# Filler matmuls kept to the first microseconds, other places for two early loads, and value rows copied from on-chip tiles

## The chip, the cores and the metric

The kernel runs on one core of a Trainium2 chip. The metric is the device time of one execution in microseconds (us); three executions of the kernel before took 718.28, 718.65 and 720.03 us, so its median is 718.65 us. The core has a matrix engine (PE, whose weight loads are listed apart as PEld), a vector engine (DVE), a scalar engine (ACT), a general engine (POOL) and a queue engine (SP), which issues nearly all the transfers (DMAs) between memory and the chip here. Each engine takes its own instructions strictly in the order in which they were written; semaphores order the engines against each other.

## The reference

Local attention with a few global keys is followed by a gated two-layer network. Shapes: 4 batches, 8 heads, 768 positions, 64 elements in a head; 8 global keys and a window of 96; then 3072 tokens of 512 elements, with 2048 hidden elements.

```python
scores = scale * q @ k^T                       # per batch and head
keep   = (pos_k < n_global) | (0 <= pos_q - pos_k < n_local)
bias   = -slope[head] * (n_local if global and not local else |pos_q - pos_k|)
a      = softmax(where(keep, scores + bias, -1e9))
x      = (a @ v) as [3072, 512]
h      = x @ w_in                              # w_in, w_out are float64 in memory
out    = (h * sigmoid(h)) @ w_out
```

Only keys in the window and the first 8 count, so a block of 128 queries needs its own 128 keys, the 96 before them and the 8 global ones: 232 columns, or 128 for the first block of a batch.

## The kernel before

The work is cut into 24 blocks of 128 queries (6 a batch) and each block into 4 pairs of heads. Two blocks form a group of 256 tokens, which goes through the network in 16 steps of 128 hidden elements; so there are 12 groups. Keys and queries of a block are loaded as rows and turned on PE (L464, "tq"), and ACT copies the turned halves out of PSUM to KHw and QHw (L534, L536). POOL copies the key columns that two blocks share (L544, L546). For each pair of heads PE makes the scores (L557 in the first 6 blocks, L529 later), DVE adds the bias and takes the extreme (L567), ACT takes the exponential and its sum (L575), DVE makes the inverse and scales (L582 to L591), PE turns the result (L605), ACT copies it out (L619), and PE multiplies by the values (L633). ACT and DVE split the attention's output in a high and a low part (xh L651, xl L654).

The network's weights come as 64-bit floats. They are staged in 32 pieces (even numbers w_in, odd ones w_out, L380), and DVE makes 32-bit floats of each with three passes over bits (L384, L390, L396) and, after ACT's high part (L403), a low part (L407). The network is then three matmuls for every product, high by high, high by low and low by high (L769 for w_in, L794 for w_out), with ACT and DVE between them (L775, L779, L783, L787). The groups 0 and 1 go through the network while the weights are still being converted. Blocks 6 and later wait for the last piece of weights.

The order of all instructions on all engines is laid down before the program is built, by a list planner (class Plan). It keeps a clock of its own with costs given by hand, takes the ready operation of lowest rank on each engine, and checks room in the pools: 3 buffers of tag "qkn" (rows of keys and queries), 3 of "big" (staged weights, later outputs), 2 each of "vn" and "vp" (values). What it writes down is a fixed order. Where its PE has nothing ready before its time WEND and a PSUM bank is free, it writes a filler, a 128x256 bf16 matmul of zeros whose result nobody reads (L905). Up to its time COLD it counts every PE cost twice.

The values that a block needs from the block before it (96 rows) and of the global keys (8 rows) are in a tile of their own, vp, filled by two DMAs (L456, L459) from v in memory. The block's own values are in vn (L449).

Of the kernel before, what the change touches and what calls it, by code (L numbers as in the profile page):

```python
# [21 lines left out]
P = 128  # L22
NPREV = 96
NG = 8
WIN = NPREV + NG + P
C1 = NPREV + NG
# [1 line left out]
FAR = 1.0e9  # L28
PAR = dict(

    LAT=140, SD=125, DL=1900, D0=2700, DW=2900, DO=3400, MG=60, T2=45000, LAT2=230, MG2=400, F0=600, F1=1200, C1=900, C2=2300, COLD=5200, WEND=60000,

    CAP=dict(po=4, av=2, s=4, h=3, tp=2, tq=4), HU=13,

    C0=14, CR=1, LW=1, LB=5, QB=3.5, RI=0.1, RN=0, RP=0.2, RM=0, RV=1.2, RQ=0.1, RB=3, LK=-25, LAG=1,

    BP=(4, 3), NX=20, CF=2, AHEAD=5, SB=(4,), CN=4, I0=6, QS='ACT',
)


# [130 lines left out]
def attn_moe(ctx, tc, q, k, v, n_global, n_local, w_in, w_out, out):  # L171
    nc = tc.nc
# [4 lines left out]
    NJ = S // P  # L177
# [148 lines left out]
    op = plan.op  # L326
# [113 lines left out]
    blk = [dict() for _ in range(B * NJ)]  # L440
    xt = {}

    def load(i, nm, h0=0, h1=H):
        b, j = divmod(i, NJ)
        pool, tag = (sb2, "vn") if nm == "v" else (sb3, "qkn")
        if not h0:
            blk[i][nm] = pool.tile([P, H, D], F32, name=f"{nm}n", tag=tag)
        src = dict(k=k, q=q, v=v)[nm]
        nc.sync.dma_start(  # L449
            blk[i][nm][:, h0:h1], src[b, h0:h1, j * P:(j + 1) * P, :].rearrange("h p d -> p h d")  # L450
        )

    def load_prev(i):
        b, j = divmod(i, NJ)
        blk[i]["vp"] = x = sb2.tile([C1, H, D], F32, name="vp")
        nc.sync.dma_start(  # L456
            x[:NPREV], v[b, :, j * P - NPREV:j * P, :].rearrange("h p d -> p h d")
        )
        nc.sync.dma_start(x[NPREV:], v[b, :, :NG, :].rearrange("h p d -> p h d"))  # L459

    def turn(i, nm, tp, p0=0, p1=NHP):
        blk[i]["t", nm, p0] = ps = bank(tp, NHP, P)
# [199 lines left out]
    before = {}  # L662
    for i in range(B * NJ):
# [13 lines left out]
                        later.append(o)  # L677
                    ob[nm + "h", p0, p1] = op("ACT", 51 + 107 * n, rank, (lambda nm=nm, a=p0, b=p1: high(0, nm, a, b)), [o], [tp, hi])
        for nm in "kq" if i else "":
            xn, tp = Buf("qkn"), Buf("tq")  # L680
            hi, lo = kk[nm.upper() + "H"], kk[nm.upper() + "L"]
            o = op("DMA", 1456, rank - lr, (lambda i=i, nm=nm: load(i, nm)), (), [xn], PAR["DL"])
            if i == PAR["I0"]:
                before["lent"] = before["move"]
            o = op("PE", 440, rank, (lambda i=i, nm=nm, tp=tp: turn(i, nm, tp)), [o, before.get("lent")], [xn, tp, hi] if whole(i) else [xn, tp, hi, lo])
            if i >= PAR["I0"]:
                hs = [op("ACT", 500, rank, (lambda i=i, nm=nm, a=a: stack_high(i, nm, a, False)), [o], [tp, x])
                      for a, x in enumerate((hi, lo))]
                for a, x in enumerate((hi, lo)):
                    y = x if nm == "k" else kk["R"]  # L690
                    ob[nm, a] = op("DVE", 718, rank, (lambda i=i, nm=nm, a=a: stack_low(i, nm, a)),
                                   hs + ([o_wf] if nm == "q" else []), [tp, x, y])
                    if nm == "q":
                        ob[nm, a, 2] = op(
                            "ACT", 640, rank + PAR["RQ"], (lambda i=i, a=a: twin_low(i, a)), [ob[nm, a]], [y]
                        )
                        ob[nm, a, 1] = op(
                            PAR["QS"], dict(ACT=628, POOL=1930, DVE=335)[PAR["QS"]], rank + PAR["RQ"],
                            (lambda i=i, nm=nm, a=a: stack_high(i, nm, a, True)), [hs[a]], [x]
                        )  # L700
                continue
            ob[nm + "h"] = op("ACT", 583 if nm == "q" else 470, rank, (lambda i=i, nm=nm: high(i, nm)), [o], [tp, hi])
# [9 lines left out]
                    )  # L712
        o_v = [op("DMA", 1456, rank - lr + 1, (lambda i=i: load(i, "v")), (), [kk["vn"]], PAR["DL"])]
        if j:
            o_v.append(op("DMA", 1183, rank - lr + 1, (lambda i=i: load_prev(i)), (), [kk["vp"]], PAR["DL"]))
        pav = Buf("av")
        last, o_m, pts = None, [], []
        for hp in range(NHP):
# [362 lines left out]
```

## Time and profile before

| What | us |
|---|---|
| median of three executions | 718.65 |
| the profiled execution | 718.39 |
| its span, first to last instruction | 716.4 |
| PE busy | 708.4 |
| DVE busy | 475.8 |
| ACT busy | 419.2 |

Around the span lie 2.0 us of the profiled execution. The page's slices of a fortieth (17.9 us) show DVE at 6 tenths in the first, 9 in the next six and 7 to 8 in the three after; from the eleventh slice on it is at 5 to 7 tenths until the last fifth. PE has 9 tenths or more in all slices but the last. A matmul's end in the trace is modelled and consecutive matmuls overlap, and fillers count as busy, so PE's share is not a share of useful work. In a window row "PE 2.00 (x12)" is busy time in that stretch and the number of instructions; in the chain of waits a row is start, length and what held the chain then; in a timeline row the bracket is the engine's idle time before and what ended it.

### The profile page before, as it was taken

What the parts mean: (1) busy time and instruction counts of PE and PEld (TensorE: products, weight loads), DVE (VectorE), ACT (ScalarE), POOL (GpSimd) and SP (SyncE); (2) the same over time, 40 slices, a digit from 0 to 9 for tenths busy, and PEclk for the clock granted to TensorE, in tenths of its full rate; (3) what the DMA queues carried; (4) which work ended last, traced back from release to release, by engine and by line L of the source; (5) the groups of instructions that cost most, each with busy time, mean ns of one, the idle gap of its engine ahead of it and who ended that gap; (6) DMA issues with size and microseconds to landing.
All of it is one profiled execution on the core that took longest, in us unless ns stands there. A gap on an engine that the chain in (4) does not pass through costs nothing.

```text
span 716.4 us, 14026 instructions
## 1 busy us (share of the span) xinstructions
PE 708.4 (99%) x5165; PEld 632.7 (88%) x5165; DVE 475.8 (66%) x1489; ACT 419.2 (59%) x1092; POOL 25.2 (4%) x83
## 2 busy tenths in 40 slices
PE   9999999999999999999999999999999999999996
PEld 7778999889999999999999998999899999998985
DVE  6999999787666757666666666665675766543332
ACT  5977444596656647556566575665664756443221
POOL 2000000010000000000000000000000000000000
PEclk9999999999999999999999999999999999999999
DMA  8895546252413305124123142240431412000001
GB/s 160 225 278 151 173 131 193 70 149 59 116 45 101 87 30 145 46 71 128 48 76 104 43 115 73 73 115 16 118 85 32 130 31 57 30 1 1 30 1 34
DMA packets 117215, 63.95 MB, mean 89 GB/s; under 512 B 93460, under 2 KB 110100, under 8 KB 117140
## 3 DMA queue, kind: packets, MB, share of 16 engines
q1 hardware_dynamic: 116992, 62.86, 32.8%
q8 instruction: 42, 0.69, 0.4%
q14 instruction: 33, 0.27, 0.1%
q10 hardware_dynamic: 148, 0.13, 0.1%
HBM read 56.69 MB, written 6.29 MB: 88 GB/s over the span
## 4 chain that ended last, share of the span: by engine, by line
PE 95%; DVE 3%; ACT 1%; issue 0%; ACTq 0%
PE bank L769 38%; PE bank L794 38%; PE bank L633 5%; PE bank L605 5%; PE bank L529 4%; PE bank L464 3%; PE bank L905 1%; PE bank L557 1%; DVE pe L591 1%; DVE pe L567 1%; ACT pe L575 1%; DVE xl L654 0%; DVE rs L582 0%; DVE wf L390 0%; DVE wf L396 0%
## 5 line engine op out<-in xcount | busy, mean ns | idle before, releaser
L769 PE MATMUL bank<-xh,WIH 128*128 128x256 f32 x768 | 224.2, 292 | 0.0
L769 PE MATMUL bank<-xl,WIH 128*128 128x256 f32 x768 | 216.1, 281 | 0.0
L769 PE MATMUL bank<-xh,WIL 128*128 128x256 f32 x768 | 215.0, 280 | 0.0
L769 PEld LDWEIGHTS bank<-xh,WIH 128*128 128x128 f32 x768 | 144.6, 188 | 10.0 <-issue 3.1
L769 PEld LDWEIGHTS bank<-xl,WIH 128*128 128x128 f32 x768 | 144.7, 188 | 6.4
L769 PEld LDWEIGHTS bank<-xh,WIL 128*128 128x128 f32 x768 | 144.8, 189 | 0.0
L794 PE MATMUL bank<-WOH,gh 128*128 128x512 f32 x336 | 135.5, 403 | 0.0
L775 ACT ACTIVATE th<-bank 128x256 f32<-128x256 f32 x192 | 73.6, 383 | 104.8 <-PE bank L769 96.2
L794 PE MATMUL bank<-WOH,gl 128*128 128x512 f32 x336 | 132.4, 394 | 0.0
L794 PE MATMUL bank<-WOL,gh 128*128 128x512 f32 x336 | 132.1, 393 | 0.0
L783 ACT CAST gh<-th 128x256 fp32r<-128x256 f32 x192 | 77.3, 402 | 83.1 <-PE bank L794 63.9
L779 DVE SCALAR_TENSOR_TENSOR th<-th,bank 128x256 f32<-128x256 f32 x192 | 80.9, 421 | 57.6 <-ACT th L775 55.6
L787 DVE TENSOR_TENSOR gl<-th,gh 128x256 fp32r<-128x256 f32 x192 | 82.0, 427 | 51.9 <-ACT gh L783 48.0
L575 ACT ACTIVATE pe<-pe,NM 128x232 f32<-128x232 f32 (+1 forms) x192 | 90.6, 473 | 32.9 <-DVE NM L567 31.1
L567 DVE CUSTOM_DVE_ANT_0 pe<-bank,B 128x232 f32<-128x232 f32 (+1 forms) x192 | 68.6, 376 | 54.6 <-PE bank L529 52.4
L794 PEld LDWEIGHTS bank<-WOH,gl 128*128 128x128 f32 x336 | 63.1, 188 | 15.2
L794 PEld LDWEIGHTS bank<-WOH,gh 128*128 128x128 f32 x336 | 63.4, 189 | 7.2 <-issue 0.5
L794 PEld LDWEIGHTS bank<-WOL,gh 128*128 128x128 f32 x336 | 63.4, 189 | 6.8
L619 ACT COPY pt<-bank 128x512 f32<-128x512 f32 (+1 forms) x80 | 43.8, 549 | 29.5 <-PE bank L605 29.2
L591 DVE TENSOR_SCALAR pe<-pe,rs 128x232 f32<-128x232 f32 (+1 forms) x192 | 56.3, 330 | 1.6
L605 PE MATMUL bank<-ident,pe 128*128 128x128 f32 (+1 forms) x352 | 55.0, 275 | 0.0
L427 DVE TENSOR_REDUCE TOP<-c 128x1 f32<-128x512 int16 x64 | 42.8, 681 | 12.2 <-DMA c<-in_moe_w_in_dram 12.2
(126 smaller groups left out, 883.2 us busy)
## 6 DMA issues: line engine op xcount, KB each, us to landing
c<-in_moe_w_in_dram SPq DMA_DIRECT2D x16, 512.0 KB, 4.8
c<-in_moe_w_out_dram SPq DMA_DIRECT2D x16, 512.0 KB, 3.9
vn<-in_v_dram SPq DMA_DIRECT2D x24, 256.0 KB, 3.7
w<-in_moe_w_in_dram SPq DMA_DIRECT2D x12, 512.0 KB, 4.7
w<-in_moe_w_out_dram SPq DMA_DIRECT2D x12, 512.0 KB, 3.6
kn<-in_k_dram SPq DMA_DIRECT2D x23, 256.0 KB, 3.7
qn<-in_q_dram SPq DMA_DIRECT2D x23, 256.0 KB, 3.1
out_dram<-osb SPq DMA_DIRECT2D x23, 256.0 KB, 2.8
```

Of the source, the lines that this page charges most:

```text
L427: nc.vector.tensor_reduce(TOP[:, i, n:n + 1], top, AX.X, (ALU.min, ALU.max)[i], apply_absolute_value=True)
L567: nc.vector.tensor_tensor_reduce(t["p", hp][:, a, :n], t["s", hp][a][:, :n], B1[:, hp] if i % NJ else B0[:, hp], -SC / (1 + a), 3.0e38, AL ...
L575: nc.scalar.activation(x, x, AF.Exp, bias=NM[:, i * H + h:i * H + h + 1], scale=-1.0, accum_out=t["sum", hp][:, a:a + 1],)
L591: nc.vector.tensor_scalar(x, x, t["inv", hp][:, a:a + 1], None, ALU.mult)
L605: nc.tensor.transpose(ps[:n, c, a], pe[:, a, c0:c0 + n], ident)
L619: nc.scalar.copy(t["pt", hp][:, c], t["tp", hp][:, c])
L769: nc.tensor.matmul(ph, w[:, c, fs], x[:, c], start=not c and not n, stop=c == NCC - 1 and n == 2)
L775: nc.scalar.activation(th, mo["ph", g, f], AF.Tanh, scale=0.5)
L779: nc.vector.scalar_tensor_tensor(gf, gf, 1.0, mo["ph", g, f], ALU.add, ALU.mult)
L783: nc.scalar.copy(gh, mo["th", g, f])
L787: nc.vector.tensor_sub(gl, mo["th", g, f], mo["gh", g, f].bitcast(F32))
L794: nc.tensor.matmul(po, a[:, s], w_o(w, f), start=f == 0 and n == 0, stop=f == NFC - 1 and n == 2)
```

## The change

Four edits, in one list of numbers and two functions. (1) WEND goes from 60000 to 8600 and COLD from 5200 to 8000 on the planner's clock, in ns. (2) The queries of blocks 1 and 2 take buffers of tag "big" instead of "qkn" (LQ). (3) vp is no longer loaded from memory: its 96 rows are copied by DMA from the last 96 rows of the preceding block's vn, and its 8 global rows from the first block's vn or the preceding block's vp. (4) In the plan this copy is an operation of 750 instead of 1183, which must follow the preceding block's value loads and keeps the preceding block's vn and vp taken until it is done.

```diff
-    ... T2=45000, LAT2=230, MG2=400, F0=600, F1=1200, C1=900, C2=2300, COLD=5200, WEND=60000,
+    ... T2=45000, LAT2=230, MG2=400, F0=600, F1=1200, C1=900, C2=2300, COLD=8000, WEND=8600,
...
-    BP=(4, 3), NX=20, CF=2, AHEAD=5, SB=(4,), CN=4, I0=6, QS='ACT',
+    BP=(4, 3), NX=20, CF=2, AHEAD=5, SB=(4,), LQ=(1, 2), CN=4, I0=6, QS='ACT',
...
+    def in_kind(i, nm):
+        return "big" if nm == "q" and i in PAR["LQ"] else "qkn"
...
-        pool, tag = (sb2, "vn") if nm == "v" else (sb3, "qkn")
+        pool, tag = (sb2, "vn") if nm == "v" else (sb3, in_kind(i, nm))
...
     def load_prev(i):
-        b, j = divmod(i, NJ)
+        j = i % NJ
         blk[i]["vp"] = x = sb2.tile([C1, H, D], F32, name="vp")
-        nc.sync.dma_start(
-            x[:NPREV], v[b, :, j * P - NPREV:j * P, :].rearrange("h p d -> p h d")
-        )
-        nc.sync.dma_start(x[NPREV:], v[b, :, :NG, :].rearrange("h p d -> p h d"))
+        old = blk[i - 1]
+        nc.sync.dma_start(x[:NPREV], old["v"][P - NPREV:])
+        nc.sync.dma_start(x[NPREV:], old["v"][:NG] if j == 1 else old["vp"][NPREV:])
...
-            xn, tp = Buf("qkn"), Buf("tq")
+            xn, tp = Buf(in_kind(i, nm)), Buf("tq")
...
-            o_v.append(op("DMA", 1183, rank - lr + 1, (lambda i=i: load_prev(i)), (), [kk["vp"]], PAR["DL"]))
+            o_v.append(op("DMA", 750, rank - lr + 1, (lambda i=i: load_prev(i)), before["v"],
+                          [kk["vp"], kb[i - 1]["vn"], *((kb[i - 1]["vp"],) if j > 1 else ())], PAR["DL"]))
+        before["v"] = o_v
```

The new numbers make the planner write another order for the first part of the program. Without the fillers, PE's matmuls stand in the same sequence in both programs from about the 650th row of the list of matmuls on (of some 4,200 of the usual path), DVE's instructions from about the 390th. Fillers go from 71 to 14.

SP's queue after the first block's four loads, before. kn_131 and qn_189 are keys and queries of block 1, kn_235 and qn_266 of block 2, kn_309 and qn_331 of block 3; vn_148 and vn_161 are values of blocks 0 and 1; vp_216 and vp_290 belong to blocks 1 and 2.

```order
L449 DMA kn_131<-in_k_dram 128x8x64
L449 DMA vn_148<-in_v_dram 128x8x64
L449 DMA vn_161<-in_v_dram 128x8x64
L449 DMA qn_189<-in_q_dram 128x8x64
L456 DMA vp_216<-in_v_dram 96x8x64
L459 DMA vp_216<-in_v_dram 8x8x64
L449 DMA kn_235<-in_k_dram 128x8x64
L449 DMA qn_266<-in_q_dram 128x8x64
L456 DMA vp_290<-in_v_dram 96x8x64
L459 DMA vp_290<-in_v_dram 8x8x64
L449 DMA kn_309<-in_k_dram 128x8x64
L449 DMA qn_331<-in_q_dram 128x8x64
```

The same place now: qn_148 and qn_242 are queries of blocks 1 and 2, kn_205 and kn_265 keys of blocks 2 and 3, vn_161 and vn_184 values of blocks 0 and 1.

```order
L453 DMA kn_131<-in_k_dram 128x8x64
L453 DMA qn_148<-in_q_dram 128x8x64
L453 DMA vn_161<-in_v_dram 128x8x64
L453 DMA vn_184<-in_v_dram 128x8x64
L453 DMA kn_205<-in_k_dram 128x8x64
L461 DMA vp_228<-vn_161 96x512
L462 DMA vp_228<-vn_161 8x512
L453 DMA qn_242<-in_q_dram 128x8x64
L453 DMA kn_265<-in_k_dram 128x8x64
L461 DMA vp_295<-vn_184 96x512
L462 DMA vp_295<-vp_228 8x512
L453 DMA qn_311<-in_q_dram 128x8x64
```

The queries of block 1 moved ahead of two loads of values, and the keys of block 2 ahead of the first vp; each vp reads a tile that a DMA ahead of it in the queue fills.

PE behind the first block's first scores, before. KHw_140 and QHw_145 are block 0's, KHw_198 and QHw_270 block 1's; pe_167 is the first pair of heads. The rows ahead of these are the turns of block 0's other heads and of block 1's keys, and ten fillers.

```order
L557 MATMUL bank0_82<-KHw_140,QHw_145 128x128
L557 MATMUL bank1_83<-KHw_140,QHw_145 128x128
L557 MATMUL bank2_84<-KHw_140,QHw_145 128x128
L557 MATMUL bank3_85<-KHw_140,QHw_145 128x128
L605 MATMUL bank4_86<-ident_72,pe_167 128x128 x2
L905 LDWEIGHTS wx_98
L905 MATMUL bank0_82<-wx_98 128x256
L557 MATMUL bank5_87<-KHw_140,QHw_145 128x128
L557 MATMUL bank6_88<-KHw_140,QHw_145 128x128
```

After these come 8 fillers, the turn of block 1's queries (qn_189), a filler, a turn of the second pair, 6 fillers and another turn, before block 1's first scores. The same place now, where qn_148 is block 1's queries and KHw_195 and QHw_202 are block 1's:

```order
L467 MATMUL bank7_89<-ident_72,kn_131 128x128 x4
L467 MATMUL bank0_82<-ident_72,qn_148 128x128 x4
L560 MATMUL bank1_83<-KHw_140,QHw_145 128x128
L560 MATMUL bank2_84<-KHw_140,QHw_145 128x128
L608 MATMUL bank3_85<-ident_72,pe_164 128x128 x2
L560 MATMUL bank4_86<-KHw_140,QHw_145 128x128
L560 MATMUL bank5_87<-KHw_140,QHw_145 128x128
L560 MATMUL bank6_88<-KHw_140,QHw_145 128x128
L560 MATMUL bank7_89<-KHw_140,QHw_145 128x128
L560 MATMUL bank0_82<-KHw_195,QHw_202 128x232
L560 MATMUL bank1_83<-KHw_195,QHw_202 128x232
```

The turn of block 1's queries now stands ahead of block 0's other scores, and block 1's first scores stand right behind these, with no filler.

ACT between block 1's keys and its first exponentials, before (pt tiles are turned weights of attention, pe_295 is block 1's first pair):

```order
L536 COPY KHw_198<-bank7_89 128x4x128
L575 ACTIVATE pe_212,sm_213<-pe_212,NM_81 128x128
L619 COPY pt_231<-bank4_86 128x256
L575 ACTIVATE pe_212,sm_213<-pe_212,NM_81 128x128
L575 ACTIVATE pe_223,sm_224<-pe_223,NM_81 128x128 x2
L575 ACTIVATE pe_238,sm_239<-pe_238,NM_81 128x128 x2
L534 ACTIVATE QHw_270<-bank7_89,twice_94 128x512
L619 COPY pt_282<-bank0_82 128x256
L619 COPY pt_q_288<-bank1_83 128x256
L619 COPY pt_q_303<-bank4_86 128x256
L575 ACTIVATE pe_295,sm_296<-pe_295,NM_81 128x232 x2
```

And now, where pe_251 is block 1's first pair:

```order
L539 COPY KHw_195<-bank7_89 128x4x128
L537 ACTIVATE QHw_202<-bank0_82,twice_94 128x512
L622 COPY pt_217<-bank3_85 128x256
L578 ACTIVATE pe_210,sm_211<-pe_210,NM_81 128x128 x2
L578 ACTIVATE pe_222,sm_223<-pe_222,NM_81 128x128 x2
L578 ACTIVATE pe_232,sm_233<-pe_232,NM_81 128x128 x2
L578 ACTIVATE pe_251,sm_252<-pe_251,NM_81 128x232
L622 COPY pt_268<-bank4_86 128x256
L578 ACTIVATE pe_251,sm_252<-pe_251,NM_81 128x232
```

The copy of block 1's queries moved ahead of six exponentials, and two of the copies of turned weights moved behind block 1's first exponentials.

More of the change, by code (lines that the diff above doesn't have):

```diff
@@ L29 @@
 PAR = dict(
-    LAT=140, SD=125, DL=1900, D0=2700, DW=2900, DO=3400, MG=60, T2=45000, LAT2=230, MG2=400, F0=600, F1=1200, C1=900, C2=2300, COLD=5200, WEND=60000,
+    LAT=140, SD=125, DL=1900, D0=2700, DW=2900, DO=3400, MG=60, T2=45000, LAT2=230, MG2=400, F0=600, F1=1200, C1=900, C2=2300, COLD=8000, WEND=8600,
     CAP=dict(po=4, av=2, s=4, h=3, tp=2, tq=4), HU=13,
     C0=14, CR=1, LW=1, LB=5, QB=3.5, RI=0.1, RN=0, RP=0.2, RM=0, RV=1.2, RQ=0.1, RB=3, LK=-25, LAG=1,
-    BP=(4, 3), NX=20, CF=2, AHEAD=5, SB=(4,), CN=4, I0=6, QS='ACT',
+    BP=(4, 3), NX=20, CF=2, AHEAD=5, SB=(4,), LQ=(1, 2), CN=4, I0=6, QS='ACT',
 )
```

## The prediction

> **What bounds the kernel now.** I read the page first, then busy time by stretches of the span.
>
> ```profile
> PE 708.4 (99%) x5165; PEld 632.7 (88%) x5165; DVE 475.8 (66%) x1489; ACT 419.2 (59%) x1092; POOL 25.2 (4%) x83
> PE 95%; DVE 3%; ACT 1%; issue 0%; ACTq 0%
> 8.00:10.00 2.00, 2.00 (x12) 1.50 (x11) 1.96 (x10) 1.32 (x4) 0.60 (x1) 1.00 1.16 217
> 10.00:12.00 2.00, 1.96 (x20) 1.32 (x18) 0.93 (x8) 0.84 (x4) 0.00 (x0) 1.00 1.27 183
> 12.00:14.00 2.00, 2.00 (x17) 1.67 (x17) 1.83 (x11) 2.00 (x11) 0.66 (x2) 1.00 1.34 217
> 14.00:16.00 2.00, 2.00 (x18) 1.48 (x15) 1.64 (x9) 1.23 (x4) 0.00 (x0) 1.00 0.78 157
> 16.00:18.00 2.00, 2.00 (x25) 1.39 (x23) 1.29 (x9) 2.00 (x9) 0.00 (x0) 1.00 0.23 51
> 18.00:20.00 2.00, 2.00 (x16) 1.20 (x14) 1.69 (x7) 1.98 (x6) 0.00 (x0) 1.00 0.88 198
> 20.00:22.00 2.00, 2.00 (x16) 1.42 (x15) 1.46 (x9) 1.63 (x6) 0.66 (x2) 1.00 0.76 158
> 22.00:24.00 2.00, 2.00 (x16) 1.19 (x14) 1.84 (x13) 2.00 (x11) 0.00 (x0) 1.00 0.64 147
> 26.00:130.00 104.00, 103.85 (x777) 89.75 (x774) 103.79 (x293) 63.88 (x168) 0.68 (x2) 1.00 0.66 188
> 134.00:700.00 566.00, 566.00 (x4146) 513.20 (x4145) 346.22 (x1080) 332.52 (x856) 19.45 (x60) 1.00 0.26 70
> ```
>
> The columns are PE, PEld, DVE, ACT, POOL. PE is always busy, but there are three regimes. From 134 on PE is full and DVE is not (346 of 566). From 26 to 130 DVE is full as well: 103.79 of 104 us. Before 24 neither DVE nor ACT is full. DVE's idle time in the seven rows from 10 to 24 is 14.00 - 10.68 = 3.32 us, and ACT's 14.00 - 11.68 = 2.32.
>
> In the middle regime PE works right behind DVE, which converts the weights:
>
> ```profile
> 87.27 0.72 DVE L407 TENSOR_TENSOR WIL<-wf,WIH 128x512 fp32r<-128x512 f32 x1
> 88.86 0.28 PE L769 MATMUL bank<-xh,WIH 128*128 128x256 f32 x1
> 132.84 0.68 DVE L407 TENSOR_TENSOR WIL<-wf,WIH 128x512 fp32r<-128x512 f32 x1
> 134.57 0.28 PE L769 MATMUL bank<-xh,WIH 128*128 128x256 f32 x1
> ```
>
> Each pair is the low part of a piece of w_in and the first matmul of that step: 0.87 us from 87.99 to 88.86, and 1.05 us from 133.52 to 134.57, so at the last piece too. PE can therefore be ahead of today's times at 134 only by as much as DVE is, and a few tenths more. After 134 the sequence on PE is the same in both programs, and PE is full: whatever is won at 134 arrives at the end unchanged. So the question is how much of DVE's 3.32 us goes.
>
> **The change, part by part.** *Fillers.* 57 of 71 go. The chain of waits shows what they take:
>
> ```profile
> 1.26 2.74 PE bank L905 x12
> 6.25 2.33 PE bank L464 x10
> 8.58 1.79 PE bank L905 x10
> 11.96 1.03 PE bank L905 x8
> 13.95 0.66 PE bank L905 x6
> 40.91 1.06 PE bank L905 x8
> 49.27 0.78 PE bank L905 x7
> 52.07 0.65 PE bank L905 x5
> ```
>
> The last six rows sum to 5.97 us for 44 of the 57; the other 13 at 1.03/8 = 0.13 us make 1.7. The most that their absence can give is thus 7.7 us. But a filler gives time only where the matmul behind it was ready. Behind the ten at 8.58 stand the scores of block 0's other pairs, whose query copy was ready earlier:
>
> ```profile
> 8.28 0.56 ACT L534 ACTIVATE QHw<-bank,twice 128x384 f32<-128x384 f32 x1
> 10.30 0.71 PE L557 MATMUL bank<-KHw,QHw 64*128 64x128 f32 x8
> 11.16 0.40 ACT L575 ACTIVATE pe<-pe,NM 128x128 f32<-128x128 f32 x1 [1.84 <-DVE NM L567]
> ```
>
> Copied by 8.84, used at 10.30, while ACT idled for 1.84 us until the first result of these scores: here fillers were in the way. The twenty from 40.91 to 52.07 (2.49 us) stand in the regime in which DVE is full; taking them out lets PE arrive early at DVE's next result. I count them as nothing; without that cover they are worth up to 2.5.
>
> *Queries of block 1 and 2.*
>
> ```profile
> 2.84 0.55 SPq L449 DMA_DIRECT2D kn<-in_k_dram  x1
> 3.42 2.12 SPq L449 DMA_DIRECT2D vn<-in_v_dram  x2
> 7.12 0.37 SPq L449 DMA_DIRECT2D qn<-in_q_dram  x1
> 12.83 0.60 PE L464 MATMUL bank<-ident,qn 128*128 128x128 f32 x4
> 13.75 0.67 ACT L534 ACTIVATE QHw<-bank,twice 128x512 f32<-128x512 f32 x1
> kn<-in_k_dram SPq DMA_DIRECT2D x1, 256.0 KB, 4.5
> vn<-in_v_dram SPq DMA_DIRECT2D x1, 256.0 KB, 5.2
> ```
>
> Block 1's queries are issued at 7.12, when a buffer comes free, and turned at 12.83. The last two rows are the landings of the load issued at 2.84 (at 7.3) and of the second vn, issued at 4.45 (9.7): two loads later, so 1.2 us a load. Issued in the place of the first vn, the queries land near 8.5. The four turns of block 1's keys end at 8.4 (ten turns from 6.25 take 2.33), so PE waits some 0.2 us, then takes 4 x 0.23 = 0.9: until 9.5. Behind that turn stand block 0's other scores, at 9.5 instead of 10.30, and block 1's first scores near 11, once block 0's are through. Both vn land 1.2 later, near 9.7 and 10.9; their first use is
>
> ```profile
> 16.74 0.66 PE L633 MATMUL bank<-pt,vn 128*64 128x128 f32 x8
> ```
>
> which hides it with 5 us to spare. The staged weights lose two buffers of "big" for that time, but in both programs SP reaches the first of them only behind the keys of block 5, by when block 2's queries are turned; so I count nothing.
>
> *Copies of value rows.* Each vp leaves 208 KB out of memory's queue; at 1.2 us for 256 KB that is about 1 us for each of blocks 1 and 2, in the only stretch where the DMA share is above 1 (the rows from 8 to 14). No row shows a copy within the chip. As ends I take nothing and the 1.2 us of a vn of 256 KB; it is nearer a load that moves fewer bytes, so below 1. The copy adds a wait on SP: for block 0's values, near 9.7, where SP would have gone on at 7.5. Queued behind it are block 2's queries, issued near 10.9 instead of
>
> ```profile
> 9.46 0.86 SPq L449 DMA_DIRECT2D qn<-in_q_dram  x1
> ```
>
> Now they land near 14.7, at the 5.2 of the vn row. Then they have ahead of them in the queue the keys of block 2 (second vn at 10.9, so 12.1), a vp of at most 1.2, and themselves 1.2: near 14.5. PE's turn of them stands behind three pairs of block 1, which begin near 11 and take ACT about 1 us each; so it may wait a few tenths. Ends: nothing, and 0.5; I take nothing, since later work on ACT lies in between. Later copies read values that were loaded a block earlier.
>
> *The sum, on ACT*, which carries more work than DVE between 10 and 22. Today:
>
> ```profile
> 14.32 0.36 ACT L619 COPY pt<-bank 128x256 f32<-128x256 f32 x1
> 14.86 0.37 ACT L619 COPY pt_q<-bank 128x256 f32<-128x256 f32 x1 [0.18 <-PE bank L605]
> 15.82 0.37 ACT L619 COPY pt_q<-bank 128x256 f32<-128x256 f32 x1 [0.59 <-PE bank L605]
> 16.09 0.49 ACT L575 ACTIVATE pe<-pe,NM 128x232 f32<-128x232 f32 x1
> ```
>
> Three terms up to block 1's exponentials: the scores come 0.8 earlier, less 0.25 that ACT then waits for them behind its query copy: 0.55. The copy of block 1's queries (13.75 to 14.32: 0.57) moves ahead of the six exponentials into the 1.84 us in which ACT now idles. The two waits of 0.18 and 0.59 vanish, since block 1's scores are there: 0.77. Together 1.9. The 0.37 of idle ACT time in the row 20 to 22 should go too: 2.3 us. DVE follows ACT there, and its bound of 3.32 holds this. So DVE enters its full regime 2.3 us earlier, PE passes 134 2.3 us earlier, and the execution of 718.39 becomes 716.1. The median lies 0.26 above that execution, which gives **716.3 us**. The bounds: nothing gained, 718.65; all of DVE's idle time and 1 us of PE's distance behind it, 4.3, so 714.3.
>
> **The clock.** PE's pace is 2.74/12 = 0.23 us a filler at the start and 1.03/8 = 0.13 at 11.96; the ten turns at 6.25 also take 0.23 each. The ten fillers at 8.58 take 1.79: five at 0.23 and five at 0.13. So the rise falls near 9.7, among fillers that go, after 3.5 us in which PE ran without a gap. The Trainium skill (TensorE: Matmul & The Clock Gate, Part 1) says that the matrix clock starts at half rate and is released after about 3.4 us of sustained activity, seen in a free-running window, and that an idle window brings it down again. The trace agrees with the first half; whether a gap of some tenths postpones the release no run here shows.
>
> **The rivals.** *A: PE alone is the bound*, so all removed fillers pay: 718.65 - 7.7 = 711. For it speaks that the chain is 95% PE; against it, that DVE is full from 26 to 130 and PE uses pieces 0.9 to 1.0 us after they are made. Chance 0.08, with anything below 714.6.
>
> *B: most of the gain is eaten at the front.* The gap near 8.4 restarts the 3.5 us: full pace at 12.1 instead of 9.7, so 2.4 us of PE at half pace, which cost up to 2.4/2 = 1.2; block 2's queries may add their few tenths. What is left is 1.2 us or less: 717.4 to 718.6. Chance 0.20.
>
> *C, slower: PE stays at half pace through the first blocks' attention.* Fillers kept PE dense: of the 12 us from 10 to 22, 1.03 + 0.66 and a few single ones, some 2 us. If the density that is left doesn't raise the clock before 22, up to 10 us of real matmuls take 20 in a stretch that is now 12: 8 lost, less the 2.3, so about 724; it decides if full pace comes after roughly 15, where half of that loss has eaten the lead. Against it: at half pace PE would hardly have gaps, and that is what came before today's rise. Chance 0.09.
>
> *D: it doesn't do what it says.* The copies' waits on SP and the reordering bring new waits, and block 1's exponentials come as late as now: 718.2 to 721. Chance 0.05.
>
> **How the numbers follow.** The forecast (a lead of 1.2 to 4 us, 714.6 to 717.4, likeliest 716.3) gets the other 0.58. A measurement of this kernel tells about 0.3% from no change, so faster means below 716.5: 0.38 of the 0.58, and A's 0.08, make 0.46. Slower, above 720.8, is C and a part of D: 0.11. The same keeps 0.43. The range 713.7 to 719.0 leaves out C, most of D and of A: 0.2.
>
> **What would show it.** Right: block 0's second scores near 9.5, block 1's first exponentials near 14, DVE's idle time between 10 and 24 near 1 us, the low part of the last piece of w_in done near 131.2 instead of 133.52, and PE full from 134 with the end at 714. A shows as PE leading DVE by less than 0.5 at L769 with the last piece near 128. B and C show in the pace of the turns: 0.23 a turn after 10. Gaps on SP before L461 beyond 2.5 us, with block 2's turn waiting for its queries, show D. Wrong altogether would be an early front whose lead is gone by 134.

## The result, and the profile after

The changed kernel takes 715.0 us (median of five executions, 714.75 to 716.37), against 718.28 to 720.03 for the kernel before: a ratio of 0.995, 95% interval 0.9936 to 0.9964. By the ratio that is 3.6 us less, 0.5%, and more than the 0.3% that the prediction took as the least that can be told; by the medians it is 4.4 us (719.44 for the five executions of the kernel before that ran beside it). Later executions of the kernel before spread wider than these five, from 716.77 to 720.58. Three executions far off all others are left out of every time here: one of 1151.07 us at a mean granted clock of 0.556, of the kernel with the fillers alone below, and two of the kernel before, of 1482.94 and 2449.01 us. The profiled execution went from 718.39 to 714.75, its span from 716.4 to 712.7.

The page of the changed kernel, busy time and the chain of waits:

```profile
PE 701.2 (98%) x5108; PEld 626.0 (88%) x5108; DVE 475.1 (67%) x1489; ACT 419.5 (59%) x1092; POOL 25.4 (4%) x83
PE 93%; DVE 5%; ACT 1%; issue 0%; DVEq 0%
```

PE has 57 instructions and 7.2 us of busy time less, but the span is only 3.7 us shorter: PE's time without work rose from 716.4 - 708.4 = 8.0 us to 712.7 - 701.2 = 11.5. So half of what the fillers took came back as waiting. Busy time by stretches of the changed kernel (PE, PEld, DVE, ACT, POOL) shows where:

```profile
8.00:10.00 2.00, 1.46 (x10) 0.99 (x10) 2.00 (x11) 2.00 (x6) 0.72 (x2) 1.00 1.20 214
10.00:12.00 2.00, 1.53 (x17) 1.14 (x16) 1.70 (x15) 2.00 (x11) 0.66 (x2) 1.00 0.86 185
12.00:14.00 2.00, 1.75 (x12) 1.17 (x12) 2.00 (x15) 1.95 (x10) 0.00 (x0) 1.00 0.93 212
14.00:16.00 2.00, 1.69 (x13) 1.08 (x11) 2.00 (x15) 2.00 (x9) 0.66 (x2) 1.00 1.13 242
16.00:18.00 2.00, 2.00 (x24) 1.58 (x23) 1.27 (x8) 2.00 (x7) 0.00 (x0) 1.00 1.02 189
18.00:20.00 2.00, 2.00 (x17) 1.44 (x16) 1.75 (x6) 2.00 (x9) 0.00 (x0) 1.00 0.59 129
20.00:22.00 2.00, 2.00 (x17) 1.37 (x18) 1.93 (x13) 2.00 (x8) 0.00 (x0) 1.00 0.71 160
22.00:24.00 2.00, 1.90 (x22) 1.27 (x24) 1.97 (x11) 2.00 (x7) 0.77 (x2) 1.00 1.12 257
26.00:130.00 104.00, 102.37 (x730) 87.75 (x728) 103.83 (x285) 63.17 (x159) 1.01 (x2) 1.00 0.62 181
134.00:700.00 566.00, 566.00 (x4140) 513.31 (x4137) 345.77 (x1081) 332.23 (x856) 19.46 (x60) 1.00 0.25 70
```

From 8 to 24 us ACT is now full: its idle time there fell from 16.00 - 13.00 = 3.00 us to 0.05, DVE's from 3.36 to 1.38. PE has gaps there, and 1.6 us more between 26 and 130, where DVE is full as before (103.83 of 104). From 134 on PE is full, as before. The first rows of PE, ACT's row of block 1's first exponential, and the last piece of w_in, from the timeline of the changed kernel (start, length):

```profile
7.18 0.66 PE L467 MATMUL bank<-ident,kn 128*128 128x128 f32 x4 [0.42 <-DMA kn<-in_k_dram]
8.38 0.66 PE L467 MATMUL bank<-ident,qn 128*128 128x128 f32 x4 [0.55 <-DMA qn<-in_q_dram]
9.19 0.49 PE L560 MATMUL bank<-KHw,QHw 64*128 64x128 f32 x4 [0.16 <-ACT QHw L537]
10.03 1.50 PE L560 MATMUL bank<-KHw,QHw 64*128 64x128 f32 x16
12.87 0.49 ACT L578 ACTIVATE pe<-pe,NM 128x232 f32<-128x232 f32 x1
129.50 0.68 DVE L407 TENSOR_TENSOR WIL<-wf,WIH 128x512 fp32r<-128x512 f32 x1
131.10 0.28 PE L774 MATMUL bank<-xh,WIH 128*128 128x256 f32 x1
```

Block 1's queries are turned at 8.38 instead of 12.83, and the exponentials of block 1 begin at 12.87 instead of 16.09. The last piece is converted at 130.18, 3.34 us earlier, and used 0.92 us later (before 1.05). From there the lead goes through unchanged. It can be read on one family of instructions that stands in the same order in all kernels: the 288 matmuls of the stacked scores, from 147 to 641 us in the kernel before. Each fence is the first of them, of the kernel before and of the changed kernel:

```profile
146.84 0.22 PE L529 MATMUL bank<-KH,QH 128*128 128x128 f32 x1
```

```profile
143.38 0.22 PE L532 MATMUL bank<-KH,QH 128*128 128x128 f32 x1
```

That is 3.46 us; at the last of the 288 it is 640.69 - 637.25 = 3.44. In what follows "the lead" of a profile is this difference at the last of them, against the kernel before's first profile. The last is needed: in six of the other profiles (fillers alone, queries alone, changed without copies, both without queries, without queries and start fillers) the instructions between the first of the 288 still stand in another order, and their lead settles only from 180 us on.

One thing in these rows isn't the change's doing. In the prediction's rows the ten turns at 6.25 took 0.23 us each; here four take 0.66 at 7.18. The trace's record of PE's granted clock begins with the rise to full pace, at 5.42 us here and at 9.88 in the kernel before, although PE's instructions up to 6 us are the same. (The clock's column in the stretches, the third number from the end, prints 1.00 for the time ahead of the record's first entry; that PE runs at half pace there shows in the lengths of its matmuls, 0.23 us a filler at the start against 0.13 later.) What the earlier rise is worth is the first thing that the experiments had to settle.

### The profile page after: what moved, and what is told of

Its sections match the earlier page's. It is cut to its first block, busy times and chain, and to the rows that moved or that the text cites. A ratio compares the mean times of both kernels' runs of the same rounds, so it can differ in the third digit from the quotient of the medians.

```text
span 712.7 us, 13915 instructions
## 1 busy us (share of the span) xinstructions
PE 701.2 (98%) x5108; PEld 626.0 (88%) x5108; DVE 475.1 (67%) x1489; ACT 419.5 (59%) x1092; POOL 25.4 (4%) x83
## 4 chain that ended last, share of the span: by engine, by line
PE 93%; DVE 5%; ACT 1%; issue 0%; DVEq 0%
PE bank L774 38%; PE bank L799 38%; PE bank L636 5%; PE bank L608 5%; PE bank L532 4%; PE bank L467 2%; DVE pe L570 1%; DVE pe L594 1%; ACT pe L578 1%; DVE wf L390 0%; PE bank L560 0%; PE bank L910 0%; DVE xl L657 0%; DVE wf L396 0%; DVE wf L384 0%; ACT QHw L537 0%
## 5 line engine op out<-in xcount | busy, mean ns | idle before, releaser
L608 PEld LDWEIGHTS bank<-ident,pe 128*128 128x128 f32 (+1 forms) x352 | 41.3, 136 | 12.5 <-DVE pe L594 4.3
```

Source lines behind the costliest of these rows:

```text
L608: nc.tensor.transpose(ps[:n, c, a], pe[:, a, c0:c0 + n], ident)
```

## The experiments

Lead and clock of every profile, and the times beside the kernel before on the same chip. A lead in brackets is the one that stood before a later step took some of it; for the repeat of the kernel before and the kernel without start fillers the step is a late transfer, as the repeat explains. The ratio goes by all executions of both kernels; where the times stand in two groups it isn't the quotient of the medians.

| Kernel | clock full from, us | lead, us | median, us | ratio, 95% interval |
|---|---|---|---|---|
| before, first profile | 9.88 | 0 | 718.65 | |
| before, again | 4.38 | 0.72 (1.34) | | |
| changed | 5.42 | 3.44 | 715.0 | 0.995 (0.9936 to 0.9964) |
| fillers alone | 4.37, half from 11.20 to 18.02 | 1.28 | 716.88 | 0.9984 (0.9969 to 1.0) |
| queries alone | 10.30 | 1.88 | 715.95 | 0.9965 (0.9952 to 0.9979) |
| copies alone | 10.24 | 0.38 | 716.79 | 0.9983 (0.9974 to 0.9992) |
| changed without copies | 10.31 | 3.37 | 714.36 | 0.9945 (0.9932 to 0.9958) |
| changed, all fillers back | 4.87 | 2.71 | 715.51 | 0.9962 (0.9948 to 0.9975) |
| changed, late fillers back | 9.31 | 2.88 | 715.31 | 0.9959 (0.9942 to 0.9975) |
| changed, ten early fillers back | 10.56 | 1.51 | 716.48 | 0.997 (0.9956 to 0.9983) |
| changed without queries | 4.73 | 3.21 | 715.33 | 0.9975 (0.9957 to 0.9993) |
| the same again | 4.29 | 3.44 | | |
| changed without start fillers | 8.76 | 2.87 (3.56) | 716.5 | 0.998 (0.9969 to 0.9991) |
| without queries and start fillers | 20.30 | -0.47 (-0.08) | 717.28 | 0.9986 (0.9971 to 1.0001) |

**The kernel before once more**, with no edit.

> The kernel before, profiled once more, unchanged. In the ten profiles so far the granted clock rises either at 4.4 to 5.4 us (four of them) or at 9.3 to 10.6 (six), never between, though the first 16 matmuls are the same in all. Theory (the clock's moment is a matter of the execution, not of the change): the rise falls in one of the same two stretches; if it is the early one, the ten turns from 6.25 on take 0.13 instead of 0.23 each and the execution takes 716.8 to 717.6 us instead of 718.4. Rival 'the change made the rise early': again 9.9 us within 0.7, as in the kernel before's first profile.

It took 717.71 us, 0.1 above the theory's range, with the clock up at 4.38. Its timeline of PE:

```profile
6.04 0.55 PE L464 MATMUL bank<-ident,qn 128*128 128x128 f32 x3
7.17 0.66 PE L464 MATMUL bank<-ident,kn 128*128 128x128 f32 x4 [0.57 <-DMA kn<-in_k_dram]
7.66 1.25 PE L905 MATMUL bank<-wx 128*128 128x256 bf16 x10
8.84 0.71 PE L557 MATMUL bank<-KHw,QHw 64*128 64x128 f32 x8
145.48 0.22 PE L529 MATMUL bank<-KH,QH 128*128 128x128 f32 x1
```

The same ten fillers take 1.25 us here, against 1.79 at 8.58; block 0's other scores come at 8.84 instead of 10.30, and 1.36 us of this stand at 145.48, 1.34 still at 434. So the clock's moment belongs to the execution, and the first lead splits into 3.46 = 1.36 + 2.10: early rise against early rise (4.38 and 5.42), the change gave **2.10 us** here, from one profile of each. Of the twelve profiles with the start fillers six had the rise at 4.29 to 5.42 and six at 9.31 to 10.56. The Trainium skill (TensorE: Matmul & The Clock Gate, Part 1) says that the activity window is free-running, 3.41 us long, so that the release varies from run to run; the trace agrees that it varies for the same order of matmuls, and the two places lie some 5 us apart. The rises and falls in these records do lie on a grid of 3.41 us. Its first point after the start of the span is at 0.87 to 2.01 in the six profiles with an early rise, and at 2.48 to 3.05 or 0.00 to 0.32 in the six with a late one, without overlap. So the place of the grid, which differs from execution to execution, goes with which of the two it is; nothing here set it on purpose.

At 455 us the repeat lost 0.62 us of its 1.34. DVE's timelines, of the kernel before's first profile and of the repeat:

```profile
448.42 0.69 DVE L427 TENSOR_REDUCE TOP<-c 128x1 f32<-128x512 int16 x1 [2.00 <-DMA c<-in_moe_w_in_dram]
```

```profile
448.27 0.69 DVE L427 TENSOR_REDUCE TOP<-c 128x1 f32<-128x512 int16 x1 [3.18 <-DMA c<-in_moe_w_in_dram]
```

In the repeat PE is 1.34 us earlier and this transfer was issued 1.34 earlier (442.25 against 443.59), but DVE's wait for it ended only 0.15 earlier, 3.18 long instead of 2.00, and after it PE had 0.62 less. In the run without start fillers a wait for the same kind of transfer until 388 us (3.25 instead of 2.26 in the changed kernel) cost 0.70. So a late transfer can take back a part of a lead that PE carries unchanged otherwise.

**The fillers alone**, on the kernel before.

```diff
-    ... COLD=5200, WEND=60000,
+    ... COLD=8000, WEND=8600,
```

> The kernel before with only the planner's two numbers changed (COLD 8000, WEND 8600): 56 of 71 fillers go, block 1's queries still come at 7.12 us and the value rows still from memory. Theory (the front's lead on ACT and DVE sets the time): the ten fillers at 8.58 go (all but one), so block 0's other scores come about 1.2 us earlier than 10.30, but block 1's queries are still turned near 12.8 and ACT waits for them; what is left is 0.5 to 1.2 us, so -0.5 to -1.2 us against the kernel before, DVE's idle time between 10 and 24 us down from 3.32 to 2.2 to 2.8. Rival 'PE alone is the bound': 56 fillers of 0.13 to 0.23 us each, -7 to -8 us. Rival 'the queries do it all': 0 within 0.3 us.

By the ratio it is 1.1 us faster, within the theory's range (by the medians, 716.88 against 718.52, 1.6, above it), but for another reason. DVE's idle time between 10 and 24 was 4.30 us, more than before, and not 2.2 to 2.8. Its busy time by stretches (the last three numbers: granted clock, DMA share, GB/s):

```profile
8.00:10.00 2.00, 1.45 (x13) 0.92 (x14) 1.95 (x13) 1.48 (x4) 0.72 (x2) 1.00 1.36 219
10.00:12.00 2.00, 1.27 (x13) 0.95 (x9) 1.75 (x13) 2.00 (x12) 0.66 (x2) 0.80 1.33 185
12.00:14.00 2.00, 1.90 (x9) 1.11 (x8) 1.47 (x9) 1.65 (x6) 0.00 (x0) 0.50 1.36 215
14.00:16.00 2.00, 2.00 (x12) 1.31 (x8) 0.73 (x4) 0.91 (x4) 0.00 (x0) 0.50 1.06 152
```

PE was idle for 1.28 us between 8 and 12, in part because it waited for block 1's queries, and the clock fell to 0.50 for 6.83 us. That is the prediction's rival C, in a kernel with only one of the edits. Its times stand in two groups, seven from 715.15 to 717.29 and four from 718.78 to 719.17. The profiled execution took 716.88 at a mean granted clock of 0.992; two more have 0.992, at 716.67 and 717.29, and the other eight 0.997 to 0.999. So a fall of this kind puts an execution near 717, and nothing shows one in the four near 719.

**The queries alone**, on the kernel before.

```diff
+    ... LQ=(1, 2), ...
...
+    def in_kind(i, nm):
+        return "big" if nm == "q" and i in PAR["LQ"] else "qkn"
...
-        pool, tag = (sb2, "vn") if nm == "v" else (sb3, "qkn")
+        pool, tag = (sb2, "vn") if nm == "v" else (sb3, in_kind(i, nm))
...
-            xn, tp = Buf("qkn"), Buf("tq")
+            xn, tp = Buf(in_kind(i, nm)), Buf("tq")
```

> The kernel before with only the queries of blocks 1 and 2 in buffers of the staged weights; 53 fillers stay, the ten behind block 0's first scores among them, and the value rows come from memory. Theory (front's lead): the queries land near 8.5 us, block 1's first scores come 1 to 2 us earlier than before, but the ten fillers (1.3 to 1.8 us) still stand ahead of block 0's other scores: -1.0 to -2.0 us against the kernel before. Rival 'the fillers do it all': 0 within 0.3 us. Rival 'all or nothing' (the two edits give their gain only together): -0.3 to -0.8 us, and e1 likewise, against -3.6 us or more for both.

```profile
8.37 2.20 PE L909 MATMUL bank<-wx 128*128 128x256 bf16 x10
10.41 0.60 PE L468 MATMUL bank<-ident,qn 128*128 128x128 f32 x4
10.94 0.49 PE L561 MATMUL bank<-KHw,QHw 64*128 64x128 f32 x4
```

As the theory had it, the ten fillers still stand ahead of the turn; and the lead is 1.88 us with a late rise. The times give 2.5 us (0.9965), half a microsecond more than the theory's upper end. In the planner's order 18 fillers went as well (53 instead of 71); whether they are the difference wasn't tested.

**The copies alone**, on the kernel before, with their operation in the plan.

```diff
-        nc.sync.dma_start(
-            x[:NPREV], v[b, :, j * P - NPREV:j * P, :].rearrange("h p d -> p h d")
-        )
-        nc.sync.dma_start(x[NPREV:], v[b, :, :NG, :].rearrange("h p d -> p h d"))
+        old = blk[i - 1]
+        nc.sync.dma_start(x[:NPREV], old["v"][P - NPREV:])
+        nc.sync.dma_start(x[NPREV:], old["v"][:NG] if j == 1 else old["vp"][NPREV:])
...
-            o_v.append(op("DMA", 1183, ...
+            o_v.append(op("DMA", 750, ...
```

> The kernel before with only the shared value rows copied on the chip. Theory: the copies take nothing off the path that sets the end, 0 within 0.5 us of the kernel before. Rival 'the memory queue is the bound of the front': each of the first copies frees about 1 us of the queue for the loads behind it, block 2's queries and keys come earlier: -0.8 to -2 us. Rival 'the wait on SP for block 0's values holds up the loads behind it': +0.5 to +2 us, with SP waiting at the first copy for more than 2.5 us.

The profile shows a lead of 0.38, as the theory says; the times show 1.2 us (0.6 to 1.9), which it doesn't: they lie in the range of the rival by which the memory queue bounds the front. These are eleven executions against 22, and when their clocks rose isn't known, so it stays open. The wait on SP is 1.0 us, so the rival of a wait on SP above 2.5 us falls. What the copies are worth in the changed kernel is seen from the other side:

**The changed kernel without the copies**: the last diff taken back.

> The changed kernel with the shared value rows loaded from memory again (the fillers' numbers and the queries' places stay changed). Theory (copies worth nothing): the same as the changed kernel, -3.3 to -3.9 us against the kernel before. Rival 'the copies relieve the queue': the gain falls to -1.5 to -2.8 us, and the keys and queries of block 2 land about 1 us later than with the copies. Rival 'the copies cost something': -4.2 us or more.

The lead is 3.37 against 3.44, the ratio 0.9945 against 0.995: the copies are worth nothing that can be told here. It is the fastest of all medians, 714.36, but not told apart from the changed kernel; at 4.0 us below the kernel before by the ratio (4.2 by the medians, interval 3.0 to 4.9) a small cost of the copies isn't ruled out either. Block 2's keys are turned later without the copies (14.32 against 12.61), as the rival by which they relieve the queue has it, but the gain doesn't fall. Its clock rose at 10.31:

```profile
8.38 1.12 PE L468 MATMUL bank<-ident,qn 128*128 128x128 f32 x4
9.42 0.80 PE L561 MATMUL bank<-KHw,QHw 64*128 64x128 f32 x4
10.57 1.50 PE L561 MATMUL bank<-KHw,QHw 64*128 64x128 f32 x16
13.42 0.49 ACT L579 ACTIVATE pe<-pe,NM 128x232 f32<-128x232 f32 x1
```

At half pace until 10.31 it still has its lead. Against the kernel before's first profile, late rise against late rise, the fillers and the queries together are worth 3.37 us.

**The changed kernel with all fillers back, with the late ones, and with the ten early ones.**

```diff
-    ... COLD=8000, WEND=8600,
+    ... COLD=5200, WEND=60000,   (all)
+    ... COLD=8000, WEND=60000,   (late)
+    ... COLD=5200, WEND=8600,    (ten early)
```

> The changed kernel with the planner's two numbers as before (COLD 5200, WEND 60000): the queries' places and the copies stay, 56 fillers instead of 14, ten behind block 0's first scores and 22 between the 180th and the 234th matmul. Theory (front's lead): only the ten early ones cost, 1.0 to 1.8 us, so the gain of the changed kernel (-3.6 us against the kernel before) falls to -1.8 to -2.6 us. Rival 'PE alone is the bound': 42 fillers of 0.13 to 0.18 us, 5.5 to 7.5 us, so +2 to +4 us against the kernel before. Rival 'the queries do it all': still -3.3 to -3.9 us.

> The changed kernel with only the late fillers back (WEND 60000, COLD 8000 kept): 32 more fillers, none behind block 0's first scores, 22 of them in the stretch in which DVE is full. Theory: they fill time in which PE would wait for DVE: the same as the changed kernel within 0.5 us, -3.1 to -3.9 us against the kernel before, and PE's idle time between 30 and 40 us (1.47 us in the changed kernel) gone. Rival 'PE alone is the bound': 32 x 0.13 = 4.2 us more, so +0.6 us against the kernel before.

> The changed kernel with COLD at 5200 again and WEND at 8600: the ten fillers behind block 0's first scores come back, and no other. Theory: they stand ahead of block 0's other scores, ten x 0.13 to 0.18 = 1.3 to 1.8 us, of which the 0.5 us that PE now waits for block 1's queries is hidden: 0.8 to 1.3 us of the lead go, -2.3 to -2.8 us against the kernel before. Rival 'the gain is in the queries alone': -3.3 to -3.9 us. Rival 'these ten are the gain': 0 to -1 us.

By the ratios the three are 2.7, 2.9 and 2.2 us below the kernel before (by the medians 3.0, 3.2 and 2.1), each just outside the theory's range, by 0.2 us at most, and the first two are far from the rival by which PE alone is the bound. The rival by which the queries do it all (3.3 to 3.9 with all fillers back) is kept out by the lead of 2.71, not by the times, whose interval reaches from 1.8 to 3.7. Late fillers first, with the changed kernel's stretch from 30 to 40 us and then the same of the kernel with late fillers:

```profile
30.00:40.00 10.00, 8.53 (x62) 5.97 (x58) 10.00 (x39) 8.70 (x26) 1.01 (x2) 1.00 0.87 224
```

```profile
30.00:40.00 10.00, 9.61 (x79) 7.24 (x76) 10.00 (x38) 8.55 (x25) 0.95 (x2) 1.00 0.86 207
```

DVE is full in both, and the fillers take up most of PE's idle time, from 1.47 us down to 0.39. Of 32 x 0.13 = 4.2 us they cost 3.44 - 2.88 = 0.56 us; two profiles of one kernel (below) have leads 0.23 apart. The ten early ones cost what the clock lets them. Timelines of the kernel with these ten, and of the one with all fillers:

```profile
8.38 2.33 PE L910 MATMUL bank<-wx 128*128 128x256 bf16 x10
10.51 0.63 PE L467 MATMUL bank<-ident,qn 128*128 128x128 f32 x4
```

```profile
7.92 1.25 PE L910 MATMUL bank<-wx 128*128 128x256 bf16 x10
9.02 0.60 PE L467 MATMUL bank<-ident,qn 128*128 128x128 f32 x4
```

With a late rise they take 2.33 us, and the lead is 1.51, which is 1.86 below the 3.37 of the late rise without copies. With an early rise they take 1.25, and the lead of the kernel with all fillers, 2.71, is 0.17 below that with the late ones alone. The latter's rise was late, 9.31, but without the ten fillers a late rise costs next to nothing (leads of 3.37 above and 3.56 below, against 3.44). So the ten fillers cost most where the clock is late, from one profile of each.

**The changed kernel without the queries' places**, twice.

```diff
-    ... LQ=(1, 2), ...
+    ... LQ=(), ...
```

> The changed kernel with the queries of blocks 1 and 2 back in the three buffers of the rows (fillers' numbers and copies stay changed). Theory: block 1's queries are issued near 7.1 us and turned near 12.8 again, ACT waits for them, and what is left is the gain of the fillers alone: -0.5 to -1.2 us against the kernel before. Rival 'the queries' places matter for the clock or the queue only': -2.5 to -3.9 us.

> The kernel of e8_no_queries once more, unchanged, to see where its second group of times (four of twelve at 718.8 to 719.3 us, the others at 714.7 to 716.3) comes from. Theory (PE's gaps while it waits for block 1's queries let the clock stay or fall to half): in an execution near 719 the clock is at half for 3 to 7 us of the stretch between 9 and 18 us, in one near 715 it is full from about 5 us on without a break. Rival 'the group comes from the transfers': the clock is the same, and a DMA wait of about 4 us stands in PE's or SP's rows.

Both profiles had an early rise and leads of 3.21 and 3.44: in these executions, with the clock up, the fillers' edit beside the copies gives nearly all of the gain, and the queries next to nothing, though they are turned at 11.06 and 10.54. The theory's -0.5 to -1.2 us has fallen for them. But the twelve times stand in two groups, eight from 714.67 to 716.27 and four from 718.78 to 719.33, so that the ratio gives only 1.8 us (0.5 to 3.1), between the theory and the rival; and the repeat, 714.69 us, caught the first group again. The mean granted clock of each execution is known and tells the groups apart: the seven up to 715.36 have 0.999, the one at 716.27 has 0.993, the four near 719 have 0.997 or 0.998. So these four had no fall of the clock after its rise either, since one of 6.83 us brings the mean to 0.992; a late first rise doesn't lower the mean, which counts the time ahead of the record as full (0.997 in the profile below whose rise came at 20.30).

**The changed kernel without 11 of 12 start fillers, with and without the queries' places.** These are meant to keep the clock from rising early.

```diff
-    ... F1=1200, ...
+    ... F1=3600, ...
```

> The changed kernel without 11 of the 12 fillers at the start (F1 3600 instead of 1200; PE begins at about 3.6 us, and from there on the order is the same). Theory (the rise needs a stretch of 3.4 us of PE work before it): the early rise never happens, the clock rises at 8.9 us or later; the ten turns cost 0.1 us more each, of which PE's waits for block 1's keys and queries (1.1 us) hide most, so 0 to +0.6 us against the changed kernel, -3.0 to -3.6 us against the kernel before. Rival 'the clock then comes after 12 us': block 1's scores at half pace, +1 to +4 us against the changed kernel. Rival 'the start fillers do nothing': the same rise times as in the changed kernel, 715.0 us.

> The kernel of e8_no_queries without 11 of its 12 fillers at the start (as in e11_no_start_fillers; the order is else the same), so that the clock can't rise at 4.4 to 5.4 us. It tells where the second group of times in e8 (four of twelve at 718.8 to 719.3 us) comes from. Theory (that group is the executions in which the rise was missed, and PE's wait for block 1's queries, 0.7 to 1.5 us near 9 to 11, then puts it off): in a good part of the executions the clock rises at 12 us or later or falls back once, and these lie near 719, so the median is 717.5 to 719.5 us, 2 us or more above the 715.2 of e8's main group. Rival 'a late rise does no harm here': the rise at 8.7 to 10.6 us in all, and 715.4 to 717 as in e11.

With the queries' places, the timeline of PE:

```profile
6.47 0.85 PE L467 MATMUL bank<-ident,qn 128*128 128x128 f32 x3
7.11 1.09 PE L467 MATMUL bank<-ident,kn 128*128 128x128 f32 x4
8.29 0.86 PE L467 MATMUL bank<-ident,qn 128*128 128x128 f32 x4
9.08 0.49 PE L560 MATMUL bank<-KHw,QHw 64*128 64x128 f32 x4
```

The rise falls into the last turn, at 8.76, and the lead was 3.56 until the late transfer: a rise there costs the changed kernel nothing. Its median is 1.5 us above the changed kernel's all the same (715.37 to 718.06), more than the theory's 0.6 and in the range of the rival by which the clock comes after 12 us, so other executions fared worse than the profiled one. None has a mean clock below 0.997, so it isn't a fall; when they rose isn't known. Without the queries' places:

```profile
14.00 1.15 PE L560 MATMUL bank<-KHw,QHw 64*128 64x232 f32 x4
15.56 1.06 PE L467 MATMUL bank<-ident,kn 128*128 128x128 f32 x4
17.63 1.12 PE L636 MATMUL bank<-pt,vn 128*64 128x128 f32 x8
20.47 0.66 PE L560 MATMUL bank<-KHw,QHw 64*128 64x232 f32 x4
```

The same four scores take 1.15 us at 14.00 and 0.66 at 20.47: half pace until 20.30, in an execution of 718.96 us, and the whole lead is gone (-0.08 against 3.56 with the queries' places). The median, 717.28, is 2 us above that of the kernel with start fillers, just below the theory's range; its times reach from 715.10 to 719.70. So an execution near 719 whose clock stayed low is shown here. That the four near 719 of the kernel with start fillers are such executions is likely, but none of them was profiled. What the queries' places are worth shows best in the times of all these kernels together: of the 22 executions with the fillers' edit and the queries' places (changed, without copies, without start fillers) none is above 718.06, and of the 36 with the fillers' edit and without these places 11 take 718.78 to 719.70.

## Why the prediction was right, and where it was wrong

The sign of the gain, its place at the front and its way through to the end were right; the time was 1.3 us too high, within the range. The sum of 2.3 us was not right for its reasons: its last step equates the lead with what DVE's idle time loses, and that isn't what the rows show. That 2.3 lies near the 2.10 us of early rise against early rise is luck. Step by step:

- **"After 134 whatever is won arrives unchanged"**: right, 3.46 us at the first stacked score and 3.44 at the last. The step was silent on transfers, which took 0.62 and 0.70 in two other profiles.
- **The regimes**: right. DVE is full from 26 to 130, PE has slack there once the fillers go, and PE used the last piece 0.92 us after it was made.
- **"The rise falls near 9.7 after 3.5 us without a gap"**: wrong as a property of the kernel. It was that of one execution; the repeat of the same kernel has it at 4.38, and half of the twelve profiles near 5. The repeat is 1.36 us ahead with no edit at all. This step put a part of the run-to-run spread into the base of the sum without saying so. The 3.5 us were misread too: in the kernel before's timeline PE has no gap from 1.26 us on, so 8.6 us without a gap came before that rise. The trace therefore doesn't show what the prediction took from it, that some 3.5 us without a gap bring the rise, and rival B's restart of that time after a gap rests on the same misreading.
- **The sum, 2.3 us**: mis-sized in its first part, and short of a term in its last. Late rise against late rise the fillers and the queries gave 3.37, where the sum should have stood; with early rises the change gave 2.10. Its first part, on ACT, was too small: block 1's first exponential came 16.09 - 13.42 = 2.67 us earlier in the late rise without copies, and 3.22 in the changed kernel, where the three terms make 1.9. Of the 1.84 us that ACT waited before 11.16 they counted 0.55 + 0.57; in the changed kernel ACT is full from 8 to 12. Its last part, that the lead is what DVE's idle time loses, didn't hold. In the changed kernel DVE's idle time from the start to the end of the last piece of w_in fell from 133.52 - 125.47 = 8.05 to 130.18 - 123.97 = 6.21, so by 1.84, less than 2.3; against the repeat of the kernel before (6.81) it fell by 0.60. The other 1.50 of the 3.34 us is busy time that DVE no longer has before that piece. Of it 0.60 is one pass of a conversion, which stands ahead of the piece's low part (132.84) in the kernel before and behind it (129.50) in the changed one:

```profile
132.24 0.68 DVE L396 SCALAR_TENSOR_TENSOR wf<-w,wf 128x512 uint32<-128x512 uint32 x1
```

```profile
130.44 0.68 DVE L396 SCALAR_TENSOR_TENSOR wf<-w,wf 128x512 uint32<-128x512 uint32 x1
```

The remaining 0.9 us is spread over shorter recorded times of other DVE instructions and isn't traced.

- **"The twenty late fillers: nothing"**: nearly. 32 of them cost 0.56 of 4.2 us. The bound of 2.5 for cover that is gone was not touched.
- **The ten fillers at 8.58** as a block that scores wait behind: right, and worth 1.86 us with a late rise, 0.2 with an early one.
- **The queries**: the landing near 8.5 and the turn at 8.38 to 9.04 were right, their place in the sum not. With an early rise the kernel without them had leads of 3.21 and 3.44. What they seem to do is keep PE fed between 8 and 12 in the executions whose clock is late: 3.56 against -0.08 in one profile each without start fillers, and no executions near 719.
- **The copies: nothing**: right on top of the other edits (3.37 against 3.44). SP waits 1.6 us before the first copy, less than 2.5, and block 2's queries are issued at 11.01, as predicted (the transfer queue of the changed kernel, below). Alone on the kernel before they made the times 1.2 us shorter, which wasn't foreseen and isn't explained.

Of the rivals, A (PE alone is the bound, -7.7) falls: of 7.2 us of PE's work taken out, 3.5 came back as waiting, and the late fillers put back cost about a seventh of their time. B and C didn't happen to the profiled execution of the changed kernel. One of its five, 716.37 us, has a mean granted clock of 0.993 where the other four have 0.997 to 0.999, near the 0.992 of the profiled execution with a fall; it wasn't profiled itself. C's mechanism exists: with the fillers' edit and without the queries, the clock fell back at 11.20 in one profile (a lead of 1.28 where 3.2 to 3.4 were to be had, so 2 us) and, without start fillers too, came only at 20.30 in another (3.6 us), where the prediction put the price at 8. D is refuted by SP's rows in the timeline of the changed kernel:

```profile
6.99 0.88 SPq L453 DMA_DIRECT2D kn<-in_k_dram  x1
9.50 0.64 SPq L461 DMA_DIRECT2D vp<-vn  x1
11.01 0.39 SPq L453 DMA_DIRECT2D qn<-in_q_dram  x1
```

SP's wait is that from 7.87 to 9.50, and nothing behind it is late: block 2's queries are turned at 14.97 without a wait.

## What to carry to other kernels

A filler costs only where something ready stands behind it, and what it costs depends on whether the clock is already up: remove those in front of ready work, and keep the next loads early enough that PE doesn't starve in the first dozen microseconds, since a clock that fell there took back 2 us of the gain in one profile here, and one that rose late the whole of it in another. Before a sum is made from one profile, profile the same kernel again: here two executions differed by 1.36 us in the first 10 us, more than half of what the change was forecast to bring. Read a lead on instructions that stand in the same order in both kernels, at the first and at the last of them, and look at every step between them: here some came from an order that still differed (up to 180 us), others from a late transfer and not from the change. And check a sum made of idle time on the engine that sets the pace, by its busy time too: a change of order can move work behind the point at which the lead is read.

## What was unexpected of the hardware

- The clock rose at 4.29 to 5.42 or at 9.31 to 10.56, never between, with the same first matmuls; falls and later rises came whole multiples of 3.41 us after the first rise (in the kernel with the fillers alone up at 4.37, down at 11.20, up again at 18.02).
- A busy PE by the profile isn't enough for a rise. In the kernel before's first profile PE has no gap from 1.26 us on and the rise came at 9.88. From 13.47 to 16.89 us in the kernel without queries and start fillers PE shows no gap (scores of 64 rows and turns), yet the rise came a window later. In the kernel with the queries' places nearly only turns fill the 3.41 us before its rise at 8.76. The Trainium skill (TensorE: Matmul & The Clock Gate, Part 4) says that transposes don't count as busy time in the same way; these turns were enough. What the window does count is open.
- Gaps didn't bring the clock down at once: windows of 3.41 us with 0.97 us (changed kernel) and 1.10 us (without queries) of idle PE kept it, one with 1.43 us (fillers alone, 7.78 to 11.20) lost it.
